# Longer K transposes and a two-instruction masked sum on VectorE, in a decode kernel that streams a KV cache

## The chip, the cores and the metric

The kernel runs on one core of one Trainium2 chip. The metric is the time of one execution in device microseconds. A core has PE (TensorE, matrix products), VectorE (DVE in the profile's lines), ACT (ScalarE), POOL (GpSimd) and SP (SyncE, which here issues the large transfers). Sixteen DMA engines carry data from HBM, the chip's main memory, to SBUF, the core's working memory; PE writes its results to PSUM. The clock that PE is granted varies within an execution, and the profile reports it (in the kernel before 6 to 9 tenths of full speed over the 40 slices of the span, 0.78 on average).

## The reference, cut to what matters

```python
B, Hq, Hkv, Sk, Dh, D = 2, 16, 8, 32768, 256, 448      # one token per batch row
q = (x @ wq) -> [B, Hq, 1, Dh]
scores = einsum("bhqd,bhkd->bhqk", q, k) * Dh ** -0.5
p = softmax(scores);  o = einsum("bhqk,bhkd->bhqd", p, v)
a = o @ wo;  b = gelu(x @ w1 + b1) @ w2 + b2
g = sigmoid((x * gate_w).sum())
return g * a + (1 - g) * b
```

The K and V caches are 2 x 8 x 32768 x 256 values of 2 bytes each, 268 MB for K and as much for V. Each value is used for two query heads only. The weights are 10 MB in all.

## The kernel before

One (batch, KV head) pair is a *group*; there are 16. A group has two K tiles and two V tiles of 8.39 MB. The kernel keeps three tiles in a ring in SBUF. SP issues K and V fills in turn, each as soon as PE has finished with the tile that the slot held:

```python
for d in order:                       # WQ, W1, K0, K1, K2, V0, K3, V1, ...
    for pd in before_of[d]:
        E.wait("pe", released(pd))    # K: last score product; V: last value product
    ...
    dma(lambda e, src=src, d=d: e.dma_start(cut(slot_of[d], 0, SLOT), src), f"slot{slot_of[d]}", ("fill", d))
```

VectorE transposes a K tile in place, as 4-byte words, in eight pieces ("chunks"). PE's score products wait for two chunks at a time:

```python
def k_words(idx, blk):
    lo = blk * CR * Dh
    return cut(slot_of[("K", idx)], lo, CR * Dh).bitcast(dt.uint32)          # 128 x 2048 words
def T(idx, blk):
    if blk == 0:
        wait_fill(E, ("K", idx))
    E.ins(lambda e: e.transpose(k_words(idx, blk), k_words(idx, blk)), key=("T", idx, blk))
# PE, in S(idx):
for m in range(NCK // 2):                      # NCK = 8
    E.wait("dve", ("T", idx, 2 * m + 1))
    ...                                        # 16 matmuls of 512 columns
```

At the end of a group the value product stands in PSUM as eight blocks of 256 columns, of which each partition row needs a masked sum. VectorE makes it with a chain of eight instructions, each waiting for the one before:

```python
def do_end(g):
    ...
    for n in range(8):
        w, i = n // 2, n % 2
        ...
        p = ps_o[:, 512 * w + 256 * i:512 * w + 256 * i + 256]
        m = mask[:, 4 * i + w:4 * i + w + 1]
        if n == 0:
            ...
            E.ins(lambda e, p=p, m=m: e.tensor_scalar(o_sb[:, 0:Dh], p, m, None, op0=ALU.mult), key=("OS0", g))
        else:
            E.wait("dve", ("OS" + str(n - 1), g))
            E.ins(lambda e, p=p, m=m: e.scalar_tensor_tensor(out=o_sb[:, 0:Dh], in0=p, scalar=m,
                      in1=o_sb[:, 0:Dh], op0=ALU.mult, op1=ALU.add), key=...)
```

VectorE's program has this order, which is also the order of its work: the transposes of a K tile; after every second tile the steps of the softmax that it shares with PE and ACT; then `do_end` of the group before.

Of the kernel before, what the change touches and what calls it, by code (L numbers as in the profile page):

```python
# [5 lines left out]
dt = mybir.dt  # L6
ACTF = mybir.ActivationFunctionType
ALU = mybir.AluOpType
AX = mybir.AxisListType
# [116 lines left out]
def bass_gated_mix__gqa_block_cached__dense_activation_gelu__decode_kernel(  # L126
# [27 lines left out]
    _, Hkv, Sk, Dh = A_k_cache.shape  # L154
# [4 lines left out]
    P = 128  # L159
    R = 128  # L160
    CR = 16
    NCK = R // CR
# [3 lines left out]
    NG = Bn * Hkv  # L166
# [34 lines left out]
    with contextlib.ExitStack() as es:  # L201
# [9 lines left out]
        o_sb = sb("o_sb", [P, Dh + 1], dt.float32)  # L211
# [24 lines left out]
        mask = sb("mask", [P, 8], dt.float32)  # L236
# [10 lines left out]
        ps_o = pm("ps_o", [P, 2048], dt.float32)  # L247
# [16 lines left out]
        def grp(g):  # L264
            return g // Hkv, g % Hkv
# [16 lines left out]
        slot_of = {("WQ", 0): 0, ("W1", 0): 0}  # L282
# [24 lines left out]
        cut = lambda s, lo, n: ring[:, s * SLOT + lo:s * SLOT + lo + n]  # L307
# [8 lines left out]
        def k_view(idx):  # L316
            return cut(slot_of[("K", idx)], 0, SLOT).rearrange("p (r b a e) -> p r b a e", r=R, b=4, a=32)

        def k_words(idx, blk):
            lo = blk * CR * Dh  # L320
            return cut(slot_of[("K", idx)], lo, CR * Dh).bitcast(dt.uint32)

        def v_view(idx):
            return cut(slot_of[("V", idx)], 0, SLOT).rearrange("p (r d) -> p r d", d=Dh)
# [4 lines left out]
        def a_win(s, w):  # L329
            lo = s * P + 30 - 2 * w  # L330
            return Abd[:, lo:lo + P]

        def keep_matmul(e, o, w, x, start, stop, tile):

            return e.add_instruction(mybir.InstMatmult(  # L335
                name=f"I-{nc.next_id()}", engine=mybir.EngineType.PE, ldweights=False,
                ins=[e.lower_ap(x), e.lower_ap(w)], outs=[e.lower_ap(o)], start_tensor_calc=start,
                stop_tensor_calc=stop, tile_size=tile[0], tile_position=tile[1], bass_skip_group_check=True))
# [60 lines left out]
        def prog_pe(E):  # L399
# [72 lines left out]
            def S(idx):  # L472
                g, t = divmod(idx, NT)
                kv = k_view(idx)
                if t == 0:
                    E.wait("act", ("A", g))
                    if g >= 1:
                        E.wait("act", ("X", g - 1))
                        E.wait("dve", ("MX", g - 1))
                for m in range(NCK // 2):  # L480
                    w = t * NCK // 2 + m
                    E.wait("dve", ("T", idx, 2 * m + 1))
                    for s in range(NS):
                        for i in range(2):
                            blk = 2 * m + i
                            o = ps_s[:, 512 * i:512 * i + 512].rearrange("p (r a) -> p r a", a=32)
                            x = kv[:, blk * CR:(blk + 1) * CR, s // 2, :, s % 2]
                            st, sp = (w == 0 and s == 0), (w == NK // 2 - 1 and s == NS - 1)
                            if i == 0:
                                fn = lambda e, o=o, x=x, st=st, sp=sp, s=s, w=w: e.matmul(  # L490
                                    o, a_win(s, w), x, start=st, stop=sp, skip_group_check=True)
                            else:
                                fn = lambda e, o=o, x=x, st=st, sp=sp, s=s, w=w: keep_matmul(
                                    e, o, a_win(s, w), x, st, sp, ((P, P), (0, 0)))
                            E.ins(fn, key=(("S", idx, m) if (s == NS - 1 and i == 1) else None))
# [74 lines left out]
            def K(idx):  # L570
                S(idx)
                if idx % NT == NT - 1:
                    g = idx // NT
                    M1(g)
                    M2(g)
# [82 lines left out]
        def prog_dve(E):  # L658
# [4 lines left out]
            for i in range(2):  # L663
                E.ins(lambda e, i=i: e.tensor_reduce(mask[:, 4 * i:4 * i + 4], idv[:, i, 0:4, :, :], AX.XY, ALU.add),
                      key=("mask" if i else "mask0"))
            E.wait("dve", "sel0")
            for h in range(2):
                E.ins(lambda e, h=h: e.tensor_reduce(selw[:, 31 - h:32 - h], ident_f[:, h:P:2], AX.X, ALU.add),
                      key=("sel" if h else "sel1"))
            for i in range(2):  # L670
                src = ident_f[0:Bn, 1 - i:2 - i].to_broadcast([Bn, 16])
                E.ins(lambda e, i=i, src=src: e.tensor_scalar(grow[:, 16 * i:16 * i + 16], src, 2.0, None, op0=ALU.mult),
                      key=("gr" if i else "gr0"))
# [45 lines left out]
# [5 lines that stand above are left out]
            def softmax(g):  # L724
                E.wait("pe", ("S", (g + 1) * NT - 1, NCK // 2 - 1))
                E.ins(lambda e: e.tensor_reduce(mx[:, :], ps_s[:, :], AX.X, ALU.max), key=("MX", g))  # L726
                E.wait("pe", ("M1", g))
                E.ins(lambda e: e.tensor_reduce(  # L728
                    gmax[:, :], ps_m[0:1, C_MXT:C_MXT + P].rearrange("p (k h) -> p h k", h=2), AX.X, ALU.max),
                    key=("GM", g))  # L730
                E.wait("dve", ("GM", g))
                E.ins(lambda e: e.tensor_copy(gmx[:, :].rearrange("p (k h) -> p k h", h=2),  # L732
                                              gmax[:, :].rearrange("p (o h) -> p o h", o=1).to_broadcast([1, P // 2, 2])),
                      key=("GX", g))
                E.wait("act", ("X", g))
                E.ins(lambda e: e.tensor_copy(ls3[:, g % 3:g % 3 + 1], lsum[:, :]), key=("LS", g))  # L736
                if g >= 1:
                    E.wait("pe", ("PV", g * NT - 1))
                E.ins(lambda e: e.transpose(PT[:, :], pexp[:, :]), key=("PT", g))  # L739

            def do_end(g):
                b, kvh = grp(g)
                if g < NG - 1:
                    E.wait("pe", ("PV", g * NT + NT - 1))
                E.wait("pe", ("OT", g - 1))
                E.wait("dve", "sel")
                E.ins(lambda e: e.tensor_copy(selg[:, :], selw[:, bass.ds(E.dyn(2 * g, 2 * UNIT // NT), 32)]), key=("SG", g))
                E.ins(lambda e: e.tensor_copy(o_sb[:, Dh:Dh + 1], ls3[:, g % 3:g % 3 + 1]), key=("OL", g))
                for n in range(8):
                    w, i = n // 2, n % 2  # L750
                    if g == NG - 1 and i == 0 and w > 0:
                        if w > 1:
                            E.wait("pe", ("PV", LASTV) if w == 3 else ("PVp", w))
# [3 lines that stand above are left out]
                        E.wait("dve", "mask")  # L757
                        if g == NG - 1:
                            E.wait("pe", ("PVp", 1))
# [3 lines that stand above are left out]
                        E.ins(lambda e, p=p, m=m: e.scalar_tensor_tensor(  # L763
                            out=o_sb[:, 0:Dh], in0=p, scalar=m, in1=o_sb[:, 0:Dh], op0=ALU.mult, op1=ALU.add),
                            key=(("OS" if n == 7 else "OS" + str(n)), g))
# [1 line left out]
            gelu1()  # L767
            gelu2()
            def K(idx):
                for blk in range(NCK):  # L770
                    T(idx, blk)
                if idx % NT == NT - 1:
                    softmax(idx // NT)

            def steps(n):
                for i in range(UNIT * n, UNIT * n + UNIT):
                    K(i + LAG)
                    if i % NT == NT - 1:
                        do_end(i // NT)

            for i in range(LAG):
                K(i)
            E.loop((NTILES - LAG) // UNIT, steps, ("dve", ("PT", 0)))
            do_end(NG - 1)
            E.wait("pe", ("OT", NG - 1))
            E.ins(lambda e: e.reciprocal(rinv[:, :], ps_oa[:, Dh:Dh + 1]), key="ri")
# [55 lines left out]
```

## Time and profile before

| | before |
|---|---|
| time, median of 3 | 1273.3 us (1273.01 to 1273.58) |
| DMA queue, share of the 16 engines' span | 99.6% |
| VectorE busy | 685.8 us, 54% |
| PE busy | 698.9 us, 55% |
| K landings, mid-kernel | every 77.4 us per two K tiles and two V tiles |

First the page of the kernel before: part 1 (busy times), two rows of part 2 (40 slices of the span in tenths; the second row in GB/s), the main queue of part 3 (packets, MB, share) and the chain's summary from part 4.

```profile
PE 698.9 (55%) x4544; PEld 146.0 (11%) x2016; DVE 685.8 (54%) x528; ACT 43.7 (3%) x183; POOL 3.3 (0%) x14
DMA  9999999999999999999999999999999999999998
GB/s 404 441 434 431 429 429 435 431 439 434 431 429 435 437 431 437 435 431 429 433 439 431 437 435 429 431 433 439 431 437 433 431 431 433 439 431 433 437 423 359
q1 hardware_dynamic: 10804, 547.43, 99.6%
DMA 63%; DVE 21%; PE 13%; issue 3%; SPq 0%; another core or an unknown queue 0%
```

The DMA engines are over 90% busy in all slices but the last; neither VectorE nor PE is much over half busy. The chain of waits (followed back from the last instruction, at each step to what released it) still gives VectorE 21%, which looks like something to gain. It has to be read with care: the chain goes from a landing back to the *issue* of that fill, and an issue is released by PE after VectorE's transposes. But the fill issued then only joins a queue of fills.

How long it stands there is shown by SP's issues and VectorE's work on the timeline. Here is the kernel before around the end of one group: SP's issues (SPq) and VectorE (start, duration, operation, and in brackets how long the engine was idle and for what).

```profile
600.47 0.33 SPq L393 DMA_DIRECT2D ring<-in_A_v_cache_dram  x1
...
608.42 0.33 SPq L393 DMA_DIRECT2D ring<-in_A_k_cache_dram  x1
608.42 1.25 DVE L739 STREAM_TRANSPOSE PT<-pexp 128x1024 bf16<-128x1024 bf16 x1 [3.57 <-PE ps_o L335]
...
609.70 0.47 DVE L760 TENSOR_SCALAR o_sb<-ps_o,mask 128x256 f32<-128x256 f32 x1
610.21 3.60 DVE L763 SCALAR_TENSOR_TENSOR o_sb<-ps_o,mask,o_sb 128x256 f32<-128x256 f32 x7
617.79 17.66 DVE L722 STREAM_TRANSPOSE ring<-ring 128x2048 uint32<-128x2048 uint32 x8 [3.97 <-DMA ring<-in_A_k_cache_dram]
...
639.18 0.33 SPq L393 DMA_DIRECT2D ring<-in_A_v_cache_dram  x1
...
656.50 17.66 DVE L722 STREAM_TRANSPOSE ring<-ring 128x2048 uint32<-128x2048 uint32 x8 [21.04 <-DMA ring<-in_A_k_cache_dram]
```

The K fill issued at 608.42 us lands at 656.5 us. Of these 48 us its own transfer takes 19.35 us (77.4 us / 4); for the rest it waits behind earlier fills. The V fill issued at 639.18 us comes while the K fill ahead of it still has until 656.5 us. So the transfers have 17 us of issued work in hand here, and it is 17.1 to 17.3 us at each V issue of the rest of the kernel (10.4 us once, in the first group, while the ring fills). VectorE, in turn, waits for K's data for 4 us after a group end and for 21 us between the two K tiles of a group.

These are the costly groups of VectorE in the kernel before (count, busy us, mean ns of one, idle time before them and what ended it).

```profile
L722 DVE STREAM_TRANSPOSE ring<-ring 128x2048 uint32<-128x2048 uint32 x256 | 565.2, 2275 | 390.2 <-DMA ring<-in_A_k_cache_dram 389.9
L763 DVE SCALAR_TENSOR_TENSOR o_sb<-ps_o,mask,o_sb 128x256 f32<-128x256 f32 x112 | 54.1, 483 | 8.9 <-PE ps_o L539 5.0
L726 DVE TENSOR_REDUCE mx<-ps_s 128x1 f32<-128x1024 f32 x16 | 19.6, 1224 | 59.9 <-PE ps_s L335 59.9
```

The main group of VectorE, the transposes, is preceded by 390 us of waiting for the K transfers: VectorE is ahead of the DMA, not behind it.

### The profile page before, as it was taken

To read this page: it belongs to the slowest core of one execution; us is meant where nothing else is said; L and a number is where in the kernel's file an instruction comes from. 1 tells how busy PE (TensorE), PEld (TensorE's weight loads), DVE (VectorE), ACT (ScalarE), POOL (GpSimd) and SP (SyncE) were. 2 spreads that over 40 slices of the span, in tenths; PEclk is the share of its full clock that TensorE was granted. 3 is DMA by queue.
4 is the path that set the end of the run, shared out by engine and by line. 5 is a ranking of instruction groups with operands and counts; after the bars stand their busy time and mean duration, and the time that the engine had idled before them with its cause. 6 is when DMAs were issued, how large, how long until landed. Compare 5 with 4: busy or idle time off the path is not lost.

```text
span 1271.6 us, 8088 instructions
## 1 busy us (share of the span) xinstructions
PE 698.9 (55%) x4544; PEld 146.0 (11%) x2016; DVE 685.8 (54%) x528; ACT 43.7 (3%) x183; POOL 3.3 (0%) x14
## 2 busy tenths in 40 slices
PE   4566566644466443665544665455664437655465
PEld 3111011100011100111100111000110001111012
DVE  2875537655365563556735466453755636566341
ACT  1000000000000000000000000000000000000000
POOL 1000000000000000000000000000000000000000
PEclk9988788767887777887778887778876778877686
DMA  9999999999999999999999999999999999999998
GB/s 404 441 434 431 429 429 435 431 439 434 431 429 435 437 431 437 435 431 429 433 439 431 437 435 429 431 433 439 431 437 433 431 431 433 439 431 433 437 423 359
DMA packets 10971, 547.59 MB, mean 431 GB/s; under 512 B 1352, under 2 KB 1616, under 8 KB 1872
## 3 DMA queue, kind: packets, MB, share of 16 engines
q1 hardware_dynamic: 10804, 547.43, 99.6%
q8 instruction: 8, 0.13, 0.0%
q10 hardware_dynamic: 156, 0.01, 0.0%
q14 instruction: 3, 0.02, 0.0%
HBM read 547.43 MB, written 0.00 MB: 431 GB/s over the span
## 4 chain that ended last, share of the span: by engine, by line
DMA 63%; DVE 21%; PE 13%; issue 3%; SPq 0%; another core or an unknown queue 0%
DMA ring<-in_A_k_cache_dram 60%; DVE ring L722 19%; PE ps_o L335 4%; PE ps_s L490 3%; PE ps_s L335 3%; DMA ring<-in_A_wo_dram 3%; DVE mx L726 1%; PE ps_o L539 1%; PE ps_m L499 0%; PE ps_m L504 0%; DVE gmax L728 0%; DVE gmx L732 0%; PE ps_f L551 0%; SPq L376 0%
## 5 line engine op out<-in xcount | busy, mean ns | idle before, releaser
L722 DVE STREAM_TRANSPOSE ring<-ring 128x2048 uint32<-128x2048 uint32 x256 | 565.2, 2275 | 390.2 <-DMA ring<-in_A_k_cache_dram 389.9
L490 PE MATMUL ps_s<-ring,Abd 128*128 128x512 bf16 x1024 | 427.0, 417 | 428.7 <-DVE ring L722 428.3
L335 PE MATMUL ps_s<-ring,Abd 128*128 128x512 bf16 x1024 | 423.3, 413 | 0.0
L490 PEld LDWEIGHTS ps_s<-ring,Abd 128*128 128x128 bf16 x1024 | 106.1, 104 | 852.0 <-DVE ring L722 480.1
L335 PE MATMUL ps_o<-ring,PT 128*24 128x512 bf16 x1504 | 112.9, 408 | 0.0
L539 PE MATMUL ps_o<-ring,PT 128*24 128x512 bf16 x544 | 58.1, 427 | 12.6 <-DMA ring<-in_A_v_cache_dram 12.6
L509 PE MATMUL ps_f<-o_sb,selg 128*32 128x257 f32 x32 | 17.0, 634 | 83.5 <-DVE o_sb L763 83.5
L763 DVE SCALAR_TENSOR_TENSOR o_sb<-ps_o,mask,o_sb 128x256 f32<-128x256 f32 x112 | 54.1, 483 | 8.9 <-PE ps_o L539 5.0
L726 DVE TENSOR_REDUCE mx<-ps_s 128x1 f32<-128x1024 f32 x16 | 19.6, 1224 | 59.9 <-PE ps_s L335 59.9
L636 ACT ACTIVATE negm<-ps_m 128x1 f32<-128x1 f32 x16 | 2.7, 171 | 1156.4 <-PE ps_m L504 1156.4
L739 DVE STREAM_TRANSPOSE PT<-pexp 128x1024 bf16<-128x1024 bf16 x16 | 19.9, 1245 | 36.8 <-PE ps_o L335 36.8
L539 PEld LDWEIGHTS ps_o<-ring,PT 128*24 128x24 bf16 x544 | 14.7, 100 | 104.1 <-issue 86.9
L736 DVE COPY ls<-lsum 128x1 f32<-128x1 f32 x16 | 2.5, 154 | 31.8 <-ACT pexp L640 31.8
L630 ACT COPY Abd<-qrep 32x16 bf16 (+1 forms) x128 | 19.4, 199 | 0.6
L640 ACT ACTIVATE pexp<-ps_s,negm 128x1024 bf16<-128x1024 f32 x16 | 17.8, 1113 | 1.7
L499 PE MATMUL ps_m<-ident_f,mx 128*1 128x128 f32 x32 | 6.1, 271 | 21.1 <-DVE mx L726 21.1
L760 DVE TENSOR_SCALAR o_sb<-ps_o,mask 128x256 f32<-128x256 f32 x16 | 7.6, 475 | 17.7 <-PE ps_o L335 17.7
L509 PEld LDWEIGHTS ps_f<-o_sb,selg 128*32 128x32 f32 x32 | 2.9, 139 | 101.6 <-DVE o_sb L763 99.5
L504 PE MATMUL ps_m<-ones_f,gmx 1*128 1x1 f32 x32 | 6.0, 256 | 9.9 <-DVE gmx L732 9.9
L728 DVE TENSOR_REDUCE gmax<-ps_m 1x2 f32<-1x128 f32 x16 | 4.5, 279 | 7.5 <-PE ps_m L499 7.5
L420 PE MATMUL ps_s<-xT,ring 128*128 128x2 bf16 x128 | 3.6, 165 | 8.1 <-DMA ring<-in_A_wq_dram 8.1
L504 PEld LDWEIGHTS ps_m<-ones_f,gmx 1*128 1x128 f32 x32 | 4.7, 183 | 14.6 <-DVE gmx L732 14.6
(76 smaller groups left out, 64.1 us busy)
## 6 DMA issues: line engine op xcount, KB each, us to landing
ring<-in_A_v_cache_dram SPq DMA_DIRECT2D x1, 4096.0 KB, 27.0
ring<-in_A_v_cache_dram SPq DMA_DIRECT2D x2, 2048.0 KB, 33.7
ring<-in_A_wq_dram SPq DMA_DIRECT2D x1, 3072.0 KB, 10.5
ring<-in_A_wo_dram SPq DMA_DIRECT2D x1, 1792.0 KB, 38.2
ring<-in_B_w_dram SPq DMA_DIRECT2D x1, 1568.0 KB, 34.3
ring<-in_B_w_dram SPq DMA_DIRECT2D x1, 1344.0 KB, 13.6
ring<-in_A_wo_dram SPq DMA_DIRECT2D x1, 1344.0 KB, 41.0
ring<-in_A_wq_dram SPq DMA_DIRECT2D x1, 512.0 KB, 11.3
```

Of the source, the lines that this page charges most:

```text
L335: return e.add_instruction(mybir.InstMatmult(name=f"I-{nc.next_id()}", engine=mybir.EngineType.PE, ldweights=False, ins=[e.lower_ap(x), e. ...
L490: fn = lambda e, o=o, x=x, st=st, sp=sp, s=s, w=w: e.matmul(o, a_win(s, w), x, start=st, stop=sp, skip_group_check=True)
L504: E.ins(lambda e: e.matmul(ps_m[:, C_BC:C_BC + 1], gmx[:, :], ones_f[0:1, 0:1], start=True, stop=True), key=("M2", g))
L509: E.ins(lambda e: e.matmul(ps_oa, selg[:, :], o_sb[:, :], start=False, stop=False, skip_group_check=True), key=("OT", g))
L539: fn = lambda e, o=o, x=x, wt=wt, st=st, sp=sp, j=j: e.matmul(o, wt, x, start=st, stop=sp, skip_group_check=True)
L630: E.ins(lambda e, o=o, Q=Q, c=c: e.copy(o[:, :, c:c + 2], qrep[32 * Q:32 * Q + 32, :, bass.ds(E.dyn(2 * g, 2), 2)]), key=(("A", g) if (Q = ...
L640: E.ins(lambda e: e.activation(pexp[:, :].rearrange("p (r i a) -> p i r a", r=CR, i=2), ps_s[:, :].rearrange("p (i r a) -> p i r a", i=2, ...
L722: E.ins(lambda e: e.transpose(k_words(idx, blk), k_words(idx, blk)), key=("T", idx, blk))
L726: E.ins(lambda e: e.tensor_reduce(mx[:, :], ps_s[:, :], AX.X, ALU.max), key=("MX", g))
L739: E.ins(lambda e: e.transpose(PT[:, :], pexp[:, :]), key=("PT", g))
L760: E.ins(lambda e, p=p, m=m: e.tensor_scalar(o_sb[:, 0:Dh], p, m, None, op0=ALU.mult), key=("OS0", g))
L763: E.ins(lambda e, p=p, m=m: e.scalar_tensor_tensor(out=o_sb[:, 0:Dh], in0=p, scalar=m, in1=o_sb[:, 0:Dh], op0=ALU.mult, op1=ALU.add), key= ...
```

## The change

The intent is to lighten VectorE by issuing fewer and longer instructions. Two chunks of K go into one transpose (128 of 128x4096 words in place of 256 of 128x2048). The masked sum becomes one multiply of all 2048 columns with a broadcast mask, in place in PSUM, and one sum over the eight blocks. The last group keeps its old form, because there the pieces of V arrive one by one.

```diff
         def k_words(idx, blk):
-            lo = blk * CR * Dh
-            return cut(slot_of[("K", idx)], lo, CR * Dh).bitcast(dt.uint32)
+            lo = blk * 2 * CR * Dh
+            return cut(slot_of[("K", idx)], lo, 2 * CR * Dh).bitcast(dt.uint32)
...
-                    E.wait("dve", ("T", idx, 2 * m + 1))
+                    E.wait("dve", ("T", idx, m))
...
+                if g < NG - 1:
+                    p = ps_o[:, :].rearrange("p (w i d) -> p w i d", w=4, i=2)
+                    mb = mask[:, :].rearrange("p (i w o) -> p w i o", i=2, o=1).to_broadcast([P, 4, 2, Dh])
+                    E.wait("dve", "mask")
+                    E.ins(lambda e: e.tensor_tensor(p, p, mb, ALU.mult), key=("OM", g))
+                    E.wait("dve", ("OM", g))
+                    E.ins(lambda e: e.tensor_reduce(o_sb[:, 0:Dh], ps_o[:, :].rearrange("p (n d) -> p d n", d=Dh),
+                                                    AX.X, ALU.add), key=("OS", g))
+                    return
                 for n in range(8):
...
-                for blk in range(NCK):
+                for blk in range(NCK // 2):
                     T(idx, blk)
```

## The prediction

> **What bounds the kernel.** The DMA queue. The page's queue table gives the one large queue 99.6% of the span, 547.43 MB at 431 GB/s over the span. In the chain that ended last, K's first transpose starts at a fixed beat: 656.56, 733.98, 811.42, 888.82 us, every 77.4 us; four 8.39 MB tiles cross in that time, 433.5 GB/s. [...] VectorE is 54% busy, PE 55%. The chain's 19% for the transposes is not a cost: an issue joins a queue. The issue table has 49.7 us from issue to landing for K and 36.6 us for V; a tile needs 19.35 us, so even V fills stand 17 us in the queue. A slot could be released 17 us later before the DMA engines ran dry.
>
> **What the change does, costed.**
> 1. Transposes. Eight per K tile take 17.66 us (timeline), one 2.275 us by itself, so the pitch is 2.198 us: 2048 elements at an estimated 1.04 ns plus some 65 ns. Four of double length: estimate 4.41 us each, 17.4 us per tile. Saved 0.26 us per tile, 8 us of VectorE in 32 tiles. The first score matmuls waited for two chunks already, so they start at most 0.1 us earlier after landing.
> 2. Group end. Eight instructions, 1227.32 to 1231.43 us in the timeline: 4.1 us (0.473, then seven at pitch 0.514). After: the multiply over 128x2048 in PSUM, and the sum over the same elements. The maximum over 128x1024 from PSUM takes 1.224 us; at 1.04 ns per further element a pass over 2048 is about 2.3 us. Estimate 2.35 + 0.04 + 2.29 = 4.7 us: 0.6 us longer per group, 15 groups (the last keeps the old form), +9 us. Fewer instructions, but twice the elements.
> VectorE's busy time therefore stays near 686 us (range 675 to 705).
> 3. PE, ACT and DMA: same instructions and bytes.
>
> **How much is critical.** None. In the timeline after a group end, VectorE is done at 613.81 us and waits until 617.79 us for K's next tile: 4 us of room for 0.6 us more. PE's product with o_sb ends at 614.93 us, its next score matmul starts at 622.35 us. At the end, the last group's eight instructions are unchanged, the weights' DMA lands at about 1267.9 us, and 3.7 us of output matmul, copy and store follow, which the change does not touch.
>
> **Predicted time: 1273.2 us, 8 times in 10 between 1272.2 and 1274.4.** Faster by over 2%: 0.01; within 2%: 0.98; slower by over 2%: 0.01.
>
> **What would show it.** K's landings still 77.4 us apart and the queue still 99.6%; transposes 128 of about 4.41 us; multiply about 2.35 us and sum about 2.3 us; V's time from issue to landing changed by under 1 us.
>
> **What would make it wrong.** The sum walks PSUM at a stride of 256 elements and the multiply reads and writes the same PSUM; either could run at half rate. That would cost VectorE 2 to 4 us per group, eating the 4 us of room, but still not the 17 us of the queue. [...]

1273.2 us is the time of the kernel before (1273.3 us) to 0.1 us, with nothing added or taken away, because none of the costed work was held to be critical. Its 1.04 ns per element was called an estimate and has no trace beside it. The traces of the two kernels show it: (4.413 − 2.275) us / 2048 for the transposes, and (2.291 − 1.224) us / 1024 from the maximum over 1024 elements to the sum over 2048, are 1.04 ns each. The 65 ns beside it is 60 ns by the traces (two pitches of 2.198 us less one of (17.42 − 4.413) us / 3). The half rate that it feared for the new group end did not come: both instructions took 2.29 us.

## The result, and the profile after

| | before | after |
|---|---|---|
| time, median of 6 | 1273.1 us (1272.99 to 1273.58) | 1273.38 us (1272.82 to 1273.65) |
| ratio, 95% interval | | 1.0001 (0.9988 to 1.0014) |
| VectorE busy | 685.8 us | 689.0 us |
| transposes, busy | 565.2 us | 557.6 us |
| VectorE instructions | 528 | 310 |
| DMA queue | 99.6% | 99.6% |

A ratio is the mean time of one kernel's fast runs over that of the other's of the same rounds, so it is not quite the ratio of the medians quoted beside it. The result is correct and the time is the same.

Here are the same lines of the page after the change, and VectorE's groups.

```profile
PE 700.1 (55%) x4544; PEld 146.6 (12%) x2016; DVE 689.0 (54%) x310; ACT 43.7 (3%) x183; POOL 3.3 (0%) x14
DMA  9999999999999999999999999999999999999998
q1 hardware_dynamic: 10804, 547.43, 99.6%
DMA 63%; PE 17%; DVE 16%; issue 3%; SPq 0%; another core or an unknown queue 0%
...
L722 DVE STREAM_TRANSPOSE ring<-ring 128x4096 uint32<-128x4096 uint32 x128 | 557.6, 4413 | 389.8 <-DMA ring<-in_A_k_cache_dram 389.5
L755 DVE TENSOR_REDUCE o_sb<-ps_o 128x256 f32<-128x2048 f32 x15 | 34.4, 2291 | 0.5
L753 DVE TENSOR_TENSOR ps_o<-ps_o,mask 128x2048 f32<-128x2048 f32 x15 | 34.3, 2288 | 0.0
```

Four in ten of VectorE's instructions are gone, yet its busy time went *up* by 3.2 us. The transposes gave 7.6 us. The multiply and the sum cost 2.288 + 2.291 us per group, and with the step between them 4.62 us on the timeline below (607.69 to 612.31 us), where the chain of eight took 4.11 us (609.70 to 613.81 us before). The chain's share of VectorE fell from 21% to 16% and PE's rose from 13% to 17%, with no change in time: which engine the chain passes through while a fill stands in the queue said nothing about cost here.

The timeline after the change, at the same group end, with the same columns.

```profile
607.69 2.29 DVE L753 TENSOR_TENSOR ps_o<-ps_o,mask 128x2048 f32<-128x2048 f32 x1
610.02 2.29 DVE L755 TENSOR_REDUCE o_sb<-ps_o 128x256 f32<-128x2048 f32 x1
617.69 17.42 DVE L722 STREAM_TRANSPOSE ring<-ring 128x4096 uint32<-128x4096 uint32 x4 [5.38 <-DMA ring<-in_A_k_cache_dram]
...
638.85 0.33 SPq L393 DMA_DIRECT2D ring<-in_A_v_cache_dram  x1
...
656.41 17.42 DVE L722 STREAM_TRANSPOSE ring<-ring 128x4096 uint32<-128x4096 uint32 x4 [21.29 <-DMA ring<-in_A_k_cache_dram]
```

K's tiles are taken up at 617.69 and 656.41 us, against 617.79 and 656.50 us before: the beat of the DMA, unmoved. (The group end itself began earlier in this group, because PE happened to finish its value product sooner there: VectorE waited 1.88 us for it in place of 3.57 us, and its transpose of the softmax weights began at 606.41 in place of 608.42 us.) The V fill is issued at 638.85 in place of 639.18 us. It joins the queue 0.33 us sooner, and the time from issue to landing is 0.3 us longer: 36.9 us in place of 36.6 us in the median of V fills.

### The profile page after: what moved, and what is told of

Its sections match the earlier page's. It is cut to its first block, busy times and chain, and to the rows that moved or that the text cites. A ratio compares the mean times of both kernels' runs of the same rounds, so it can differ in the third digit from the quotient of the medians.

```text
span 1271.5 us, 7780 instructions
## 1 busy us (share of the span) xinstructions
PE 700.1 (55%) x4544; PEld 146.6 (12%) x2016; DVE 689.0 (54%) x310; ACT 43.7 (3%) x183; POOL 3.3 (0%) x14
## 3 DMA queue, kind: packets, MB, share of 16 engines
q1 hardware_dynamic: 10804, 547.43, 99.6%
## 4 chain that ended last, share of the span: by engine, by line
DMA 63%; PE 17%; DVE 16%; issue 3%; SPq 0%; another core or an unknown queue 0%
DMA ring<-in_A_k_cache_dram 60%; DVE ring L722 14%; PE ps_s L490 6%; PE ps_s L335 5%; PE ps_o L335 4%; DMA ring<-in_A_wo_dram 3%; DVE mx L726 1%; PE ps_o L539 1%; PE ps_m L499 0%; PE ps_m L504 0%; DVE gmax L728 0%; DVE gmx L732 0%; PE ps_f L551 0%; SPq L376 0%
## 5 line engine op out<-in xcount | busy, mean ns | idle before, releaser
L722 DVE STREAM_TRANSPOSE ring<-ring 128x4096 uint32<-128x4096 uint32 x128 | 557.6, 4413 | 389.8 <-DMA ring<-in_A_k_cache_dram 389.5
L755 DVE TENSOR_REDUCE o_sb<-ps_o 128x256 f32<-128x2048 f32 x15 | 34.4, 2291 | 0.5
L753 DVE TENSOR_TENSOR ps_o<-ps_o,mask 128x2048 f32<-128x2048 f32 x15 | 34.3, 2288 | 0.0
L769 DVE TENSOR_SCALAR o_sb<-ps_o,mask 128x256 f32<-128x256 f32 x1 | 0.5, 484 | 15.5 <-PE ps_o L335 15.5
## 6 DMA issues: line engine op xcount, KB each, us to landing
ring<-in_A_wq_dram SPq DMA_DIRECT2D x1, 3072.0 KB, 10.4
```

Source lines behind the costliest of these rows:

```text
L753: E.ins(lambda e: e.tensor_tensor(p, p, mb, ALU.mult), key=("OM", g))
L755: E.ins(lambda e: e.tensor_reduce(o_sb[:, 0:Dh], ps_o[:, :].rearrange("p (n d) -> p d n", d=Dh), AX.X, ALU.add), key=("OS", g))
```

## The experiments

**Theory.** The DMA queue sets the time. VectorE has some 3 to 5 us of room before the K tile that follows a group end (its waits there are 3.3 to 5.4 us in the changed kernel), and behind that another 17 us while issued fills are in hand.

**Rival 1.** The time does depend on VectorE, and the two halves of the change cancel (−7.6 us and +10.9 us of busy time).

**Rival 2.** The release of ring slots through the transposes, a fifth of the chain, is a real cost.

The sum of the two halves is what makes a test necessary: a change that leaves VectorE's load nearly as it was proves nothing about VectorE by being neutral.

### Each half alone

Only the transposes and their wait (the first, second and last part of the diff above), group end as before:

> Only the transposes of two chunks each; the group end as in the kernel before. Theory (the DMA queue sets the time, VectorE has room): 1273.2 us as both kernels, ratio 0.999 to 1.001, VectorE's busy time down by some 8 us to about 678 us, K's tiles still landing 77.4 us apart. Rival 1 (the two halves of the change each move the time and cancel): 4 to 8 us faster, ratio 0.994 to 0.997. Rival 2 (the release of ring slots through the transposes, 19% of the chain, is a real cost): faster by up to 8 us.

Only the group end (the third part):

> Only the group end as one multiply in PSUM and one summing instruction; transposes of one chunk as before. Theory: 1273.2 us, ratio 0.999 to 1.001, VectorE's busy time up by some 10 us to about 697 us, VectorE's waits for K's landing shorter by as much after group ends. Rival 1 (halves cancel): 4 to 10 us slower, ratio 1.003 to 1.008.

Measured: pairs only 1273.02 us (1272.84 to 1273.85, 5 runs), ratio 0.9999 (0.9985 to 1.0012); sum only 1273.03 us (1272.83 to 1273.18, 5 runs), ratio 0.9997 (0.9984 to 1.0011). Part 1 of the two pages, pairs only first:

```profile
PE 702.7 (55%) x4544; PEld 146.7 (12%) x2016; DVE 678.2 (53%) x400; ACT 43.7 (3%) x183; POOL 3.3 (0%) x14
```

```profile
PE 700.8 (55%) x4544; PEld 146.4 (12%) x2016; DVE 696.7 (55%) x438; ACT 43.7 (3%) x183; POOL 3.3 (0%) x14
```

VectorE's busy time is 18.5 us apart in these two kernels, and the times are equal. Rival 1 falls, and with it the gain that rival 2 forecast.

### How much room there is

The sum is repeated in place, which leaves the result right and makes VectorE slower at exactly the place that the change touches:

```diff
                     E.wait("dve", ("OM", g))
+                    for k in range(4):          # 4, 8 or 20
+                        E.ins(lambda e: e.tensor_reduce(...same...), key=("OX" + str(k), g))
+                        E.wait("dve", ("OX" + str(k), g))
                     E.ins(lambda e: e.tensor_reduce(...), key=("OS", g))
```

Four more:

> The changed kernel, whole bytes, four more sums per group: 9.3 us of VectorE per group, 140 us in all, 17 times what the new group end added. The room is 5 us before K's landing plus the 17 us of the V fill in the queue, and eight more (18.6 us) cost 9 us. Theory: nothing to be seen, 1272.5 to 1274.5 us, ratio 0.999 to 1.001, V's fills after a group end issued some 4 us later against K's landings.

Eight more:

> The changed kernel with the summing instruction of a group end done nine times in place of once (the result is the same): 8 x 2.33 = 18.6 us more of VectorE in series per group, 280 us in 15 groups. Theory: hidden, because the room is about 5 us before K's next landing plus 17 us that V's fill stands in the queue: 1273 to 1276 us; VectorE over 70% busy; V's time from issue to landing down by some 13 us to about 23 us; the queue still 99% busy. Rival 2 (slot releases through VectorE cost time): slower by about 13 us per group, 190 us.

Twenty more:

> Twenty more sums per group, 46.6 us. VectorE's own round per group is, read from the changed kernel's timeline, about 52.5 us (two tiles of transposes 34.8, the softmax steps with their waits on PE and ACT about 13, the group end 4.6); with 46.6 more it is about 99 us against the 77.4 us that the DMA needs. Theory: VectorE now sets the time, 21.7 us more per group in 13 to 15 groups: 1550 to 1600 us, the DMA queue near 80%, so the method of adding work does find a limit where there is one. If the time still did not move, the added work would be no test.

| more sums | VectorE added per group | time | ratio | VectorE busy | DMA queue |
|---|---|---|---|---|---|
| 0 (the changed kernel) | 0 | 1273.38 us | 1.0001 | 689.0 us | 99.6% |
| 4 | 9.3 us | 1272.96 us (1272.90 to 1273.52, 4 runs) | 1.0000 (0.9983 to 1.0017) | 825.1 us | 99.7% |
| 8 | 18.6 us | 1282.17 us (1280.85 to 1284.80, 4 runs) | 1.0071 (1.0056 to 1.0086) | 962.6 us | 99.3% |
| 20 | 46.6 us | 1630.78 us (1 run) | | 1373.4 us | 78.3% |

The run with twenty more, a single one, was repeated for the next experiment: 1632.44 us, ratio 1.2815, queue 78.2%.

Four more sums add 136 us of VectorE work to the kernel and nothing to its time. Eight more cost 9 us out of 274 us added; the theory had 0 to 3. (At 0.7%, its interval lies clear of 1.) Twenty more make VectorE the limit. That run is longer than the 1550 to 1600 us expected: by the last group's maximum it is 326 us behind the changed kernel (1545.18 against 1219.46 us), the top of what was expected, but another 32 us come after it, because at the end of the kernel the added sums stand before the last value product with no transfer left to hide them, which the estimate had left out.

The timelines say where the room ends. First four more sums, then eight more: VectorE's last sum, the transposes of the two K tiles that follow, and SP's issue of the V fill between them.

```profile
620.54 2.29 DVE L759 TENSOR_REDUCE o_sb<-ps_o 128x256 f32<-128x2048 f32 x1
622.75 17.41 DVE L722 STREAM_TRANSPOSE ring<-ring 128x4096 uint32<-128x4096 uint32 x4
...
643.99 0.33 SPq L393 DMA_DIRECT2D ring<-in_A_v_cache_dram  x1
...
656.06 13.10 DVE L722 STREAM_TRANSPOSE ring<-ring 128x4096 uint32<-128x4096 uint32 x3 [15.90 <-DMA ring<-in_A_k_cache_dram]
```

```profile
634.23 2.29 DVE L759 TENSOR_REDUCE o_sb<-ps_o 128x256 f32<-128x2048 f32 x1
636.43 17.41 DVE L722 STREAM_TRANSPOSE ring<-ring 128x4096 uint32<-128x4096 uint32 x4
...
657.58 0.33 SPq L393 DMA_DIRECT2D ring<-in_A_v_cache_dram  x1
...
660.34 17.43 DVE L722 STREAM_TRANSPOSE ring<-ring 128x4096 uint32<-128x4096 uint32 x4 [6.49 <-DMA ring<-in_A_k_cache_dram]
```

The time from V's issue to the landing of the K tile ahead of it is the work that the DMA still has in hand. It was 17.6 us in the changed kernel (638.85 to 656.41), is 12.1 us with four more sums (643.99 to 656.06; 5.5 us less, where some 4 were expected) and 2.8 us with eight more (657.58 to 660.34). Over the groups after the first it is 11.9 to 13.7 us with four more and 2.5 to 7.0 us with eight more. The theory's 17 us of queue were real and are nearly used up there. By the end, K's last landing is 7.6 us later than in the changed kernel (1205.9 against 1198.3 us). That makes most of the 9 us; the rest arises after it, at the end of the kernel, where 18.6 us more stand before the last group. The 7.6 us come unevenly: the landings that VectorE waits for, once per group, are 77.4 to 79.9 us apart. The packet records of the two traces, between 60 and 1200 us, show two losses. A DMA engine is without a packet for some 4.7 us in all (mean of the 16), against 0.5 us in the changed kernel; and 120 packets of 64 KB take over 2.6 us (the median is 2.42 us), against 6. Why those packets are slower stays open. V's median time from issue to landing, which the theory had falling to 23 us, stayed at 36.6 us, because one V fill of each group comes early and keeps its long time (37.1 us for the one at 604.07 us). The late one shown above, at 657.58 us, does take 22.3 us. So the median was the wrong line to watch. Rival 2, which would have had 190 us, falls.

### Where VectorE does set the time

With twenty more sums VectorE's round takes about 100.7 us per group (in the repeated run its maxima come at 1142.50, 1243.20, 1343.87 us), against 77.4 us of DMA. If the theory is right, a VectorE saving shows there. The changed kernel with twenty more sums was run once more, beside the same kernel with transposes of one chunk:

> The changed kernel with twenty more sums per group once more, now timed. VectorE's round is 100.7 us of which PE has some 50 us of rest, so VectorE alone sets the time. About 1631 us.

> The same with transposes of one chunk. Theory (a VectorE saving shows in full only where VectorE alone sets the time, and PE has rest): 0.49 us more in each of 16 groups, 8 us slower than the run with pairs, 1639 us. Rival (PE's granted clock takes back any VectorE saving in every regime, as the runs with half the bytes might be read): within 2 us of it.

Measured: pairs 1632.44 us (1628.82 to 1632.88, 4 runs), ratio to the kernel before 1.2815; single chunks 1638.49 us (1636.19 to 1640.45, 4 runs), ratio 1.2875. The ratios differ by 0.0060, or 7.6 us, and the medians by 6.1 us, where 8 were expected; the ranges do not overlap. The rival's "within 2 us" falls. VectorE's round after the last sum, in the two kernels, pairs first:

```profile
1000.87 2.29 DVE L759 TENSOR_REDUCE o_sb<-ps_o 128x256 f32<-128x2048 f32 x1
1003.08 34.72 DVE L722 STREAM_TRANSPOSE ring<-ring 128x4096 uint32<-128x4096 uint32 x8
```

```profile
1002.48 2.29 DVE L759 TENSOR_REDUCE o_sb<-ps_o 128x256 f32<-128x2048 f32 x1
1004.69 35.20 DVE L722 STREAM_TRANSPOSE ring<-ring 128x2048 uint32<-128x2048 uint32 x16
```

No wait for a landing stands before the transposes any more, and the 0.48 us per group (7.7 us in 16 groups) arrives in the time, in full or nearly so. So the saving is real; in the kernel as it stands it has nowhere to go.

### Half the bytes

The other way to take the DMA off the critical path is to load less. After the first fill of each slot only the first half of each tile is loaded, and all the arithmetic runs as ever on what the slot holds; the result is wrong.

```diff
+                    n = SLOT if fill_no[d] == 1 else 64 * Dh
-                    dma(lambda e, src=src, d=d: e.dma_start(cut(slot_of[d], 0, SLOT), src),
+                    dma(lambda e, src=src, d=d, n=n: e.dma_start(cut(slot_of[d], 0, n), src[:, 0:n]),
```

> The kernel before with half the bytes: after the first fill of each ring slot only the first half of every K and V tile is loaded, and everything else runs as ever on what the slot held (a wrong result on purpose). DMA then needs some 38.7 us per group; VectorE's round without the added sums was 100.7 - 46.5 = 54.2 us in the run with twenty more sums, with waits on PE in it. Theory: the DMA queue was the limit, so the time falls to where VectorE's round sets it: 16 rounds of 54 us and some 60 us of start and end, 900 to 960 us, the queue at 70% to 78%.

> The changed kernel with half the bytes, wrong on purpose in the same way. Theory (VectorE is now on the critical path, and the change's two halves cancel there): within 3 us of the kernel before with half the bytes, because the pairs take away 0.26 us in each of 32 tiles (8.3 us) and the new group end adds 0.5 us in each of 15 groups (8 us).

> Transposes of two chunks only, group end as before, half the bytes, wrong on purpose. Theory: 6 to 9 us faster than the kernel before with half the bytes (32 tiles x 0.26 us). If PE at a lower granted clock sets the pace of the scores in its place, the gain is smaller, 0 to 4 us.

> The new group end only, transposes of one chunk, half the bytes, wrong on purpose. Theory: 6 to 9 us slower than the kernel before with half the bytes (15 groups x 0.55 us, all in VectorE's round, which the next K tile's transposes follow at once).

| half the bytes | time, 4 runs | ratio to the whole kernel before | VectorE busy | waits of VectorE for scores + for the value product |
|---|---|---|---|---|
| kernel before | 880.24 us (880.05 to 880.48) | 0.6914 | 683.2 us | 60.1 + 38.1 us |
| changed | 879.92 us (879.39 to 880.95) | 0.6912 | 686.0 us | 65.8 + 33.1 us |
| pairs only | 880.25 us (879.44 to 882.13) | 0.6911 | 675.5 us | 64.3 + 41.9 us |
| new sum only | 881.35 us (879.03 to 881.67) | 0.6923 | 693.6 us | 60.6 + 28.3 us |

Halving the bytes took 393 us away: the DMA was the limit. The new limit is about 51 us per group, shorter than the 54 us that had been carried over from the run with twenty more sums, so the 900 to 960 us expected for the kernel before were missed, and so was the queue's share (79.4%, where 70% to 78% were expected). (In that run VectorE waited about 5 us for the value product in a group; here it waits 1.9 or 3.5 us.) The expected equality of the changed kernel held. But the expected 6 to 9 us of each half alone did *not* show; only the alternative noted for the pairs, "0 to 4 us", covers what came. The lines of VectorE's waits (us in total, times, longest) say where the time went: *mx* is the maximum, which waits for the scores, and *PT* the transpose of the softmax weights, which waits for the value product. First the kernel before, then pairs only, then new sum only:

```profile
DVE mx L727 <- PE ps_s L335: 60.1, 16, 3.9
DVE PT L740 <- PE ps_o L335: 38.1, 15, 3.6
```

```profile
DVE mx L727 <- PE ps_s L335: 64.3, 16, 4.1
DVE PT L740 <- PE ps_o L335: 41.9, 15, 3.6
```

```profile
DVE mx L727 <- PE ps_s L335: 60.6, 16, 3.9
DVE PT L740 <- PE ps_o L335: 28.3, 15, 2.0
```

Against the kernel before with half the bytes, the pairs kernel saved 7.7 us of VectorE and waited 8.0 us more for PE (4.2 + 3.8). The sum kernel worked 10.4 us longer on VectorE and waited 9.3 us less for PE (0.5 us more for the scores, 9.8 us less for the value product). These sums are of one execution each, and not of typical ones: pairs only was profiled in its slowest run (882.13 us), new sum only in its fastest (879.03 us). They also leave some 2 us of each kernel's difference in span unexplained. The wait before PT takes one of two values, 1.88 or about 3.5 us (the longer one in 8 of 15 groups with pairs only, in 6 of 15 in the kernel before, in none with the new sum only), and the pace of PE's value product goes with it. Its groups of four matmuls start 0.22 us apart in a group of new sum only that waits 1.88 us, and for part of the product 0.43 us apart in a group of pairs only that waits 3.57 us. The granted clock was read beside the pace in the whole kernels: it was 1.00 from 602 to 607 us in the changed kernel (0.22 us apart, wait 1.88 us) and 0.50 from 604.56 to 606.26 us in the kernel before (0.43 us apart, wait 3.57 us). What sets the clock of a group, and so which groups wait 1.88 and which 3.5 us, no run here shows.

So there is a possible third rival: PE's clock takes back whatever VectorE gains. A last run adds two more sums to the changed kernel with half the bytes:

> The changed kernel with half the bytes and two more sums per group, 4.65 us, 70 us in 15 groups; wrong on purpose. With half the bytes the waits of VectorE on PE were near their floor in the run with the new group end only (1.89 us before PT, 3.79 us before the maximum) and above it in the run with pairs only, which is where the 8 us went. Theory: only the distance to that floor, 5 to 10 us in all, can be taken back, so the time rises by 60 to 70 us, to 940 to 950 us. Rival (PE's granted clock sets the pace, VectorE rides behind it): rises by under 35 us.

Measured: 951.26 us (950.90 to 951.53, 4 runs), just above the 940 to 950 us expected, and 71.3 us more than without them, for 70 us added. The rival (under 35 us) falls. The theory's floor, which was to give 5 to 10 us back, was not borne out either: nothing was given back, as the waits before PT rose from 33.1 to 40.2 us in all. What remains of it is this: with half the bytes VectorE and PE share the limit (busy 574 and 547 us of the 700 us from 100 to 800 us in the kernel before), VectorE's waits for PE move by plus or minus 10 us over the kernel, with the value product at one pace or the other, and an 8 us difference on VectorE was lost in that. Why PE was slower just in the pairs kernel is left open, and so is why savings and losses of 8 to 10 us were lost where 70 us added came through in full.

No version that beats both kernels came out of this. The queue is 99.6% busy with bytes that must be read; outside it lie the first 2 us or so, before the weights' first packets, and the last 3.7 us of the span, which nothing here tried to shorten.

## Why the prediction was right

- *The DMA queue bounds the kernel; K lands every 77.4 us.* Right. After the change K's first transposes are at 656.41 and, mid-kernel, every 77.4 us; the queue is at 99.6%, and halving the bytes took 31% of the time. A window of one group in the trace (578.99 to 656.41 us) moves 433 GB/s.
- *Transposes: 4.41 us each, 17.4 us per tile, 8 us saved.* Right: 4.413 us, 17.42 us, 7.6 us less busy time. The prediction doesn't say from which trace it took its 1.04 ns per element; the two kernels show it, as said under the prediction.
- *Group end: 2.35 + 0.04 + 2.29 us, 0.6 us longer.* Right: 2.288 + 0.04 + 2.291 us, 0.5 us longer. The sum at a stride of 256 elements and the multiply in place in PSUM took 2.29 us each, where half the rate would have been over 4 us (estimate from the measured 1.04 ns, 2 x 2048 x 1.04 ns); the worry about half rate was unfounded. That two passes over 2048 elements would not be the faster form could be seen from the kernel before alone, by an estimate: from 0.475 us for 256 columns of PSUM (the chain's first multiply) to 1.224 us for 1024 (the maximum) is 0.975 ns per further column, so a pass over 2048 takes about 2.2 us and two take 4.4 us, against the 4.1 us that the trace shows for the old chain.
- *VectorE near 686 us (675 to 705).* Right: 689.0 us.
- *None of it critical.* Right, and shown: each half alone, and 136 us of added VectorE work, left the time where it was.
- *A slot could be released 17 us later before the DMA ran dry.* Right as a measure of the queue (17.6 us in hand in the changed kernel), a little generous as a tolerance: adding 18.6 us, of which 5 us are absorbed before K's landing, left 2.8 us in hand in the group shown (2.5 to 7.0 us over the groups) and cost 9 us. So the loss began here while there was still some work in hand, and not only with the queue empty.
- *V's time from issue to landing within 1 us.* Right: 36.6 to 36.9 us.

## What to carry to other kernels

Before making an engine faster, find what it waits for and how much issued work stands in the queue ahead: here 390 us of VectorE's idle time ended with a landing, and 17 us of transfers were in hand at each late issue, so neither a saving nor a loss of some us could reach the time. Fewer instructions are not less work: merging saved the fixed part of an instruction (0.06 us for a transpose here, 7.6 us in 128 merges), and it lost in the sum, where the merged form passes over the elements twice (4.62 us in place of 4.11 us). And when a change is neutral, test its parts and add a known load: the equality alone can't tell "off the critical path" from "two effects that cancel".
